# Writing out the engine order ahead of the first block, and loading the first weights deeper

## Chip, cores and metric

One core of one Trainium2 chip. The metric is the device time of one execution in microseconds (us); three runs of the kernel before gave a median of 1016.64 us (1015.66 to 1017.76).

## The reference

Sparse attention over 4 batches and 8 heads of width 64, then two feed-forward networks in a row over 2304 tokens of width 512, all in fp32:

```python
s = scale * q @ k.T          # 512 local tokens: a window of +-32 and 32 global keys
a = exp(s - max(s)); a = a / (sum(a) + 1e-9); x = a @ v
h = x @ w_in;  g = where(h > 0, h, exp(min(h, 0)) - 1);  y = g @ w_out
xn = y / sqrt(mean(y * y) + 1e-6) * rms_g
out = (silu(xn @ w_gate) * (xn @ w_val)) @ w_o2
```

The 32 global tokens of each batch attend to all 544 keys. The weights arrive as 64-bit floats; the kernel gets them as 64-bit integers, turns them into fp32 on the chip, and splits each into a rounded high part and a rest, so that a product is three matmuls.

## The kernel before, in words

**Attention** works on 16 tiles of 128 local tokens, u = 0 to 15. For each, `a_S` (L189) computes scores on TensorE, takes the maxima and scales them on VectorE (L209, L210) and the exponentials on ScalarE (L212). `a_T` (L215) transposes the exponentials on TensorE and copies them on ScalarE (L220). `a_PV` (L223) multiplies with v on TensorE (L235) and divides on VectorE (L239 to L241). `a_X` (L243) transposes the four finished tiles of a block into xT, whose high part ScalarE writes (L250) and whose rest VectorE subtracts (L251).

**Blocks.** `moe_block` (L277) runs the first network over 512 tokens in 16 slots, j = 0 to 15: twelve matmuls for h (`mm1`, L115), the activation (`act1`, L119; in block 0 through `elu_a`, L102), and twelve matmuls into the output sums for the slot before (`mm2`, L129). In blocks 0 to 2 the slots also hold the attention of the four tiles of the next block (`att_slot`, L255), one step each in three slots out of four. Block 3 holds the global tokens. The second network follows.

**Weights.** Sixteen pairs of weight tiles of the first network, in the order of `order1` (L146), are each loaded raw (`dec_load`, L68, 1 MB) and decoded (`decode`, L73): an Abs on ScalarE (L76), four operations on VectorE (L77 to L80), a cast of the high part on ScalarE (L85) and a subtraction on VectorE (L86). The first h needs pairs 0 and 1, the first output sums pair 2; slot 4 needs pairs 4 and 5, slot 8 pairs 8 and 9, slot 12 pairs 12 and 13. Three pairs are decoded ahead of block 0, and one is written into each slot of it after that. The eighteen pairs of the second network (`w2_decode`, L379) are decoded without the split, stored to a DRAM tensor `wT` and read back late in block 3. Both use two buffers for raw tiles (pool `decr`) and two for decoded ones (pool `dec`, tag `dx`). The pool `wpool` has 16 buffers of tag `w`; ahead of block 0 it holds the key/query and value tiles of u = 0 to 3 (`load_kq`, `load_v`, L171 and L180) and later the 16 split weight pairs.

**Order.** TensorE's instructions run in the order in which they are written (L43). The order on VectorE, on ScalarE and of the DMA issues on SP is chosen by a scheduler, which simulates the kernel on a timeline: it gives an engine that it takes to be free the first ready instruction in the order of writing, however far ahead that one was written, if its buffers are free. The order on each engine is fixed once that is done. All loads are issued from SP.

The stretch ahead of block 0 stands at L304 to L370, the slots of block 0 at L388, those of blocks 1 and 2 at L403.

Of the kernel before, what the change touches and what calls it, by code (L numbers as in the profile page):

```python
# [39 lines left out]
def fused_kernel(ctx: ExitStack, tc: tile.TileContext, kq, vl, gkq, gv, w_in, w_out, w_gate, w_val, w_o2, rms_g, consts, out):  # L40
# [27 lines left out]
    def dec_load(pool, src):  # L68
        raw = pool.tile([P, 2, 512], I64, tag="raw", name="raw")
        nc.sync.dma_start(out=raw, in_=src)  # L70
        return raw

    def decode(pool, raw):  # L73
        x = pool.tile([P, 1024], F32, tag="dx", name="dx")
        word = raw.rearrange("p a n -> p (a n)").bitcast(I32).rearrange("p (n w) -> p n w", w=2)
        nc.scalar.activation(x, f(word[:, :, 1]), AF.Abs)  # L76
# [4 lines left out]
        return x  # L81

    def split_w(dst, t):
        t = t.rearrange("p (a n) -> p a n", a=2)
        nc.scalar.copy(dst[:, :, 0, :], t)  # L85
        nc.vector.tensor_tensor(out=dst[:, :, 1, :], in0=t, in1=f(dst[:, :, 0, :]), op=ALU.subtract)  # L86
# [73 lines left out]
    with ExitStack() as ls:  # L160
# [8 lines left out]
        kq_t, v_t, e_t, et_t, x_t = {}, {}, {}, {}, {}  # L169
# [19 lines left out]
        def a_S(u, pools):  # L189
# [12 lines left out]
            for pr in range(4):  # L202
                for par in range(2):
                    r = slice(64 * par, 64 * par + 64)
                    nc.tensor.matmul(ss[par][:, pr, 96:128], t[r, pr, 224:352], t[r, pr, 192:224], start=False, stop=(pr == 3), skip_group_check=True)
            mx = small.tile([P, 2, 4], F32, tag="st", name="mx")
# [16 lines left out]
        def a_PV(u, pools):  # L223
# [3 lines left out]
            if T == 0:  # L227
                x_t[b] = moe.tile([P, 4, 512], F32, tag="x32", name="x")
            x = x_t[b][:, T, :].rearrange("p (a e d) -> p e a d", a=4, e=2)
            os_ = [pools[i][0].tile([P, 4, 65], F32, tag=pools[i][1], name="o") for i in range(2)]  # L230
            st = small.tile([P, 2, 4, 2], F32, tag="st", name="st")
            for par in range(2):
                for pr in range(4):
                    for i in range(4):
                        nc.tensor.matmul(os_[par][32 * i:32 * i + 32, pr, :], ets[par][:, pr * P + 32 * i:pr * P + 32 * i + 32], v[:, i, 2 * pr + par, :],  # L235
                                         start=True, stop=True)
            for par in range(2):
# [17 lines left out]
        def att_slot(b, j, part):  # L255

            u, jj = 4 * (b + 1) + j // 4, j % 4
            if jj == 0 and part == 0:
                a_S(u, ATT2)
                load_kq(u + 1)  # L260
            if jj == 1 and part < 2:
                a_T(u, part, aps, "att")
            if jj == 2 and part == 0:
                a_PV(u, ATT2)
                load_v(u + 1)
# [43 lines left out]
        nc.scalar.copy(identr, ident)  # L309
        nc.scalar.copy(masks, mk)  # L310
        load_v(0)
        load_kq(1)
        nc.vector.memset(eps, 1e-6)

        raws, n_raw, n_dec = [], [0], [0]
# [7 lines left out]
        def w1_decode(n):  # L323
            for _ in range(n):
                i = n_dec[0]
                if i < 16:
                    n_dec[0] += 1
                    t = decode(dec["t"], raws.pop(0))
                    w1_load()
                    kind, a, G = order1[i]  # L330
                    dst = wpool.tile([P, 2, 2, 512], F32R, tag="w", name="wA")
                    for k in range(2):
                        if kind == "1":
                            W1[a + k, G] = dst[:, k]
                        else:
                            W2[a + k] = dst[:, k]
                    split_w(dst, t)
# [12 lines left out]
        load_kq(3)  # L350
        load_v(3)
        a_PV(0, [(yps, "y2"), (yps, "y3")])
        a_S(2, ATT2)
        a_T(1, 0, yps, "y0")
        a_T(1, 1, yps, "y1")
        w1_decode(1)
        nc.sync.dma_start(out=gcol, in_=rms_g.rearrange("(c p) -> p c", p=P))
        a_PV(1, [(yps, "y2"), (yps, "y3")])
        a_S(3, HB)
        a_T(2, 0, yps, "y0")  # L360
        a_T(2, 1, yps, "y1")
        w1_decode(1)
        a_PV(2, [(yps, "y2"), (yps, "y3")])
        a_T(3, 0, yps, "y0")
        a_T(3, 1, yps, "y1")
        a_PV(3, [(yps, "y2"), (yps, "y3")])
        xT_t = {0: new_xT()}
        a_X(0, range(4), xT_t[0], ATT2[:2] + HB)
        load_kq(4)
        load_v(4)  # L370

        raws2, n_raw2, n_dec2 = [], [0], [0]

        def w2_load():
            if n_raw2[0] < 18:
                raws2.append(dec_load(dec["r"], w_src(*order2[n_raw2[0]])))
                n_raw2[0] += 1

        def w2_decode(n):  # L379
            for _ in range(n):  # L380
                i = n_dec2[0]
                if i < 18:
                    n_dec2[0] += 1
                    t = decode(dec["t"], raws2.pop(0))
                    nc.sync.dma_start(out=wT[2 * i:2 * i + 2].rearrange("a p n -> p a n"), in_=t.rearrange("p (a n) -> p a n", a=2))
                    w2_load()

        def slot0(j, part, h):  # L388
            g = act1(h, 512, elu_a) if part == 0 else None
            att_slot(0, j, part)  # L390
            if part == 2:
                w1_decode(1)
# [3 lines left out]
                if j in (13, 15):  # L396
                    w2_decode(1)
# [17 lines left out]
        w2_decode(18)  # L415
# [408 lines left out]
```

## Time and profile before

| | |
|---|---|
| median of 3 runs | 1016.64 us |
| profiled execution | 1016.54 us, span 1014.6 us |
| TensorE matmul busy | 943.7 us, 93% of the span |
| VectorE busy | 457.6 us, 45% |
| ScalarE busy | 348.1 us, 34% |
| mean granted TensorE clock | 0.965 |

Engines are called PE (TensorE matmul), PEld (TensorE weight load), DVE (VectorE), ACT (ScalarE), POOL and SP in the profile; a name with q is the engine's queue. L12 is line 12 of the kernel. All times count from the start of the span. An instruction's row gives its start, its duration, its engine, its line, what it writes and reads, and in brackets how long the engine sat idle before it and who ended that. Clock and DMA share are fractions of the full value.

### The profile page before, as it was taken

The page shows a single profiled execution, that of the slowest core. Times are in us where ns is not written, and L with a number is a line of the kernel's source. Part 1 is how long each engine was busy: PE and PEld are TensorE (multiplying, and loading weights), DVE is VectorE, ACT ScalarE, POOL GpSimd, SP SyncE. Part 2 cuts the span into 40 slices and gives each one's busy share as a digit, 9 for nine tenths or more (in the row PEclk, how much of TensorE's full clock was granted, in tenths as well). Part 3 has the DMA queues.
Part 4 walks back from the last instruction along what each step waited for, and adds up shares of the span by engine and source line. Part 5 has one row for each costly group of instructions (what it writes and reads, how often), then busy time and mean ns, then how long its engine had stood idle before and what let it go on. Part 6 is the DMA issues. An engine that isn't in the chain of part 4 may idle for free.

```text
span 1014.6 us, 15748 instructions
## 1 busy us (share of the span) xinstructions
PE 943.7 (93%) x6738; PEld 781.1 (77%) x6738; DVE 457.6 (45%) x791; ACT 348.1 (34%) x627; POOL 23.7 (2%) x27
## 2 busy tenths in 40 slices
PE   5667898968999999999989999999999999999997
PEld 4545686757887888867777788888888999999996
DVE  3889878877534333443357611412142142142111
ACT  3555645434323232333255522311132142142111
POOL 0000000000000000010010001000100010010000
PEclk9568899989999999999999999999999999999999
DMA  9655687687222212243164400010011001000000
GB/s 354 240 172 209 199 284 276 246 302 272 93 72 69 98 60 72 99 161 125 53 211 135 156 11 1 31 42 1 1 32 42 1 1 63 1 1 32 1 1 32
DMA packets 34446, 107.78 MB, mean 106 GB/s; under 512 B 3016, under 2 KB 5704, under 8 KB 31816
## 3 DMA queue, kind: packets, MB, share of 16 engines
q1 hardware_dynamic: 34376, 106.77, 29.9%
q8 instruction: 53, 0.87, 0.4%
q14 instruction: 17, 0.14, 0.0%
HBM read 88.41 MB, written 18.35 MB: 105 GB/s over the span
## 4 chain that ended last, share of the span: by engine, by line
PE 71%; DMA 11%; DVE 10%; ACT 4%; issue 2%; SPq 1%; ACTq 0%; DVEq 0%
PE pg L561 14%; PE y L567 14%; PE pv L561 14%; PE h L115 11%; PE y L129 11%; DMA raw<-in_moe_w_out 3%; DMA raw<-in_moe_w_in 3%; DMA raw<-in_moe_w_val 3%; DMA raw<-in_moe_w_gate 2%; DVE dx L79 2%; ACT dx L76 2%; DVE dx L80 1%; PE ptp L218 1%; PE o L235 1%; DVE dx L77 1%
## 5 line engine op out<-in xcount | busy, mean ns | idle before, releaser
L129 PE MATMUL y<-g,wA 128*128 128x512 f32 x768 | 205.8, 412 | 6.5 <-ACT g L122 3.3
L115 PE MATMUL h<-xT,wA 128*128 128x512 f32 x768 | 192.6, 400 | 2.8 <-DVE xT L251 2.7
L129 PEld LDWEIGHTS y<-g,wA 128*128 128x128 f32 x768 | 144.1, 195 | 40.8 <-DVE g L123 5.0
L115 PEld LDWEIGHTS h<-xT,wA 128*128 128x128 f32 x768 | 145.9, 192 | 36.6 <-DVE xT L251 3.4
L719 DVE TENSOR_TENSOR silu<-pv,silu 128x384 f32<-128x384 f32 (+1 forms) x60 | 36.7, 611 | 262.2 <-PE pv L561 256.0
L567 PE MATMUL y<-wB,p 128*128 128x512 f32 x612 | 150.7, 393 | 0.0
L567 PEld LDWEIGHTS y<-wB,p 128*128 128x128 f32 x612 | 114.5, 188 | 23.9
L561 PE MATMUL pv<-xT,wB 128*128 128x384 f32 (+1 forms) x432 | 89.0, 354 | 0.0
L718 ACT ACTIVATE silu<-pg 128x384 f32<-128x384 f32 (+1 forms) x60 | 32.1, 534 | 161.3 <-PE pg L561 161.1
L97 DVE TENSOR_SCALAR e<-e 128x512 f32<-128x512 f32 x52 | 22.1, 424 | 134.5 <-ACT e L96 134.5
L561 PEld LDWEIGHTS pv<-xT,wB 128*128 128x128 f32 x432 | 77.7, 188 | 5.9
L721 ACT CAST p<-silu 128x384 fp32r<-128x384 f32 (+1 forms) x60 | 33.4, 557 | 125.7 <-DVE silu L719 125.4
L96 ACT ACTIVATE e<-h 128x512 f32<-128x512 f32 x48 | 28.8, 600 | 118.5 <-PE h L115 109.9
L561 PE MATMUL pv<-xnB,wB 128*128 128x512 f32 (+1 forms) x288 | 61.9, 363 | 0.0
L122 ACT CAST g<-e 128x512 fp32r<-128x512 f32 x64 | 39.7, 620 | 63.2 <-DVE e L98 49.1
L561 PE MATMUL pg<-xT,wB 128*128 128x384 f32 (+1 forms) x288 | 60.4, 358 | 0.0
L76 ACT ACTIVATE dx<-raw 128x1024 f32<-128x1024 f32 x34 | 38.9, 1145 | 61.8 <-DMA raw<-in_moe_w_out 21.4
L561 PEld LDWEIGHTS pv<-xnB,wB 128*128 128x128 f32 x288 | 52.4, 188 | 5.9
L561 PEld LDWEIGHTS pg<-xT,wB 128*128 128x128 f32 x288 | 52.1, 188 | 6.1 <-issue 0.5
L722 DVE TENSOR_TENSOR p<-silu,p 128x384 fp32r<-128x384 f32 (+1 forms) x60 | 37.5, 625 | 35.6 <-ACT p L721 35.6
L123 DVE TENSOR_TENSOR g<-e,g 128x512 fp32r<-128x512 f32 x64 | 44.1, 689 | 19.8 <-ACT g L122 19.1
L218 PE MATMUL ptp<-ident,E 128*128 128x128 f32 x128 | 26.0, 342 | 21.9 <-ACT E L212 21.8
(180 smaller groups left out, 986.5 us busy)
## 6 DMA issues: line engine op xcount, KB each, us to landing
raw<-in_moe_w_out SPq DMA_DIRECT2D x14, 1024.0 KB, 6.1
wT<-dx SPq DMA_DIRECT2D x18, 512.0 KB, 4.2
wraw<-wT SPq DMA_DIRECT2D x18, 512.0 KB, 4.0
raw<-in_moe_w_in SPq DMA_DIRECT2D x8, 1024.0 KB, 6.2
raw<-in_moe_w_gate SPq DMA_DIRECT2D x6, 1024.0 KB, 6.5
raw<-in_moe_w_val SPq DMA_DIRECT2D x6, 1024.0 KB, 8.1
gvr<-in_gv SPq DMA_DIRECT2D x8, 640.0 KB, 5.0
gkq<-in_gkq SPq DMA_DIRECT2D x4, 1152.0 KB, 5.5
```

Source lines behind the costliest of these rows:

```text
L76: nc.scalar.activation(x, f(word[:, :, 1]), AF.Abs)
L115: nc.tensor.matmul(h[:, :n], W1[c, G][:, ws, o:o + P], xT[c][:, xs, :n], start=(k == 0), stop=(k == 11))
L122: nc.scalar.copy(g[:, 0, :n], e[:, :n])
L123: nc.vector.tensor_tensor(out=g[:, 1, :n], in0=e[:, :n], in1=f(g[:, 0, :n]), op=ALU.subtract)
L129: nc.tensor.matmul(ys[dc][:, :n], W2[j][:, ws, dc * P:(dc + 1) * P], g[:, gs, :n], start=(j == 0 and k == 0), stop=(j == 15 and k == 2))
L218: nc.tensor.transpose(pt[:, pr * P:(pr + 1) * P], e_t[u][par][:, pr, :], ident)
L561: nc.tensor.matmul(ps[:, :n], W[c, G3][:, ws, o:o + P], xn[c][:, xs, :n], start=(k == 0), stop=(k == 11))
L567: nc.tensor.matmul(os_[t], p[:, pp, t * P:(t + 1) * P], Wo[j][:, ww, :], start=(j == 0 and k == 0), stop=(j == 11 and k == 2))
L718: nc.scalar.activation(s[:, :n], pg[:, :n], AF.Silu)
L719: nc.vector.tensor_tensor(out=s[:, :n], in0=pv[:, :n], in1=s[:, :n], op=ALU.mult)
L721: nc.scalar.copy(p[:, 0, :n], s[:, :n])
L722: nc.vector.tensor_tensor(out=p[:, 1, :n], in0=s[:, :n], in1=f(p[:, 0, :n]), op=ALU.subtract)
```

## The change

Line numbers after `@@` are of the kernel before.

- `a_S` keeps the scores; the softmax becomes `a_E`. `a_PV` keeps the product; the division becomes `a_N`. `decode` becomes `dec_abs` and `dec_bits`, `split_w` becomes `split_hi` and `split_lo`. What is computed, and how often, stays the same.
- The stretch ahead of block 0 is written out step by step inside a region in which VectorE and ScalarE, too, run in the order of writing. Where instructions that are written outside the region fall among them stays the scheduler's choice, and so does SP's order.
- Raw tiles 1, 3, 5, 7, 9 and 11 go to `wpool` instead of `decr`. Five raw loads are written ahead of the first decode instead of two, two more after the region, and then one after each decode.
- The second weights' decodes are written into the odd slots of blocks 1 and 2 and two more slots of block 2, none in block 0; the first two loads stay in slot 12 of block 0.

```diff
 def w1_load(n=1):
     for _ in range(n):
-        if n_raw[0] < 16:
-            raws.append(dec_load(dec["r"], w_src(*order1[n_raw[0]])))
+        i = n_raw[0]
+        if i < 16:
+            wp = i % 2 == 1 and i < 12
+            raws[i] = dec_load(wpool if wp else dec["r"], "w" if wp else "raw", w_src(*order1[i]))
             n_raw[0] += 1
...
-w1_load(1)
-load_v(1)
-w1_load(1)
-load_kq(2)
-load_v(2)
-a_S(0, ATT2)
-a_S(1, HB)
-a_T(0, 0, yps, "y0")
-a_T(0, 1, yps, "y1")
-w1_decode(1)
-load_kq(3)
-load_v(3)
-a_PV(0, [(yps, "y2"), (yps, "y3")])
...
+with tc.manual_schedule(engines={mybir.EngineType.DVE, mybir.EngineType.Activation}):
+    nc.scalar.copy(identr, ident)
+    nc.scalar.copy(masks, mk)
+    load_kq(1)
+    w1_load()
+    load_v(1)
+    w1_load()
+    load_kq(2)
+    load_v(2)
+    load_kq(3)
+    load_v(3)
+    w1_load(3)
+    a_S(0, ATT2)
+    a_E(0)
+    a_S(1, HB)
+    w1_abs(0)
+    a_T(0, 0, yps, "y0")
+    a_T(0, 1, yps, "y1")
+    w1_bits(0)
+    a_E(1)
+    a_PV(0, Y2)
+    w1_hi(0)
+    a_N(0)
+    w1_lo(0)
+    a_S(2, ATT2)
+    w1_abs(1)
+    a_T(1, 0, yps, "y0")
+    a_T(1, 1, yps, "y1")
+    a_E(2)
+    w1_bits(1)
+    a_PV(1, Y2)
+    w1_hi(1)
+    a_N(1)
+    a_S(3, HB)
+    a_T(2, 0, yps, "y0")
+    a_T(2, 1, yps, "y1")
+    a_E(3)
+    w1_lo(1)
+    a_PV(2, Y2)
+    a_N(2)
+    w1_abs(2)
+    a_T(3, 0, yps, "y0")
+    a_T(3, 1, yps, "y1")
+    w1_bits(2)
+    a_PV(3, Y2)
+    a_N(3)
+    w1_hi(2)
+    xT_t = {0: new_xT()}
+    a_X(0, (0, 1), xT_t[0], ATT2[:2] + HB)
+    w1_lo(2)
+    a_X(0, (2, 3), xT_t[0], ATT2[:2] + HB)
+w1_load(2)
 load_kq(4)
 load_v(4)
+nc.sync.dma_start(out=gcol, in_=rms_g.rearrange("(c p) -> p c", p=P))
...
 if part == 2:
-    w1_decode(1)
+    w1_decode()
     if j == 12:
         w2_load()
         w2_load()
-    if j in (13, 15):
-        w2_decode(1)
...
 if part == 2:
-    w2_decode(1 if j % 2 else 0)
+    if j % 2 or (b == 2 and j in (4, 10)):
+        w2_decode()
...
-w2_decode(18)
+assert n_dec2[0] == 18
```

## Rows read from the trace of the kernel before

**Rows 1.** Chain of waits that ended last, shares of the span by engine.

```profile
PE 71%; DMA 11%; DVE 10%; ACT 4%; issue 2%; SPq 1%; ACTq 0%; DVEq 0%
```

**Rows 2.** Busy time by stage: PE, PEld, DVE, ACT, POOL, clock, DMA share, GB/s.

```profile
12.30:65.90 53.60, 32.81 (x551) 25.00 (x550) 43.06 (x77) 29.37 (x58) 0.00 (x0) 0.65 0.69 261
65.90:121.50 55.60, 44.88 (x377) 35.80 (x378) 49.93 (x67) 31.68 (x54) 0.00 (x0) 0.84 0.58 198
121.50:194.00 72.50, 69.06 (x630) 54.83 (x628) 59.12 (x92) 38.62 (x66) 0.00 (x0) 1.00 0.79 274
194.00:262.00 68.00, 56.71 (x490) 44.39 (x489) 50.71 (x80) 25.85 (x46) 0.00 (x0) 0.92 0.73 259
...
321.00:430.90 109.90, 109.46 (x1018) 88.68 (x1017) 42.36 (x96) 35.16 (x78) 0.00 (x0) 1.00 0.23 82
```

**Rows 3.** Timeline of TensorE, first matmuls of blocks 0, 1, 2: start, us.

```profile
65.91 4.72 PE L115 MATMUL h<-xT,wA 128*128 128x512 f32 x12 [2.35 <-DVE xT L251]
...
194.00 2.81 PE L115 MATMUL h<-xT,wA 128*128 128x512 f32 x10
...
321.00 2.88 PE L115 MATMUL h<-xT,wA 128*128 128x512 f32 x12
```

**Rows 4.** Groups by line up to 66 us: busy, mean ns | idle before.

```profile
L79 DVE SCALAR_TENSOR_TENSOR dx<-raw,dx 128x1024 int32<-128x1024 int32 x7 | 8.5, 1216 | 0.0
...
L86 DVE TENSOR_TENSOR wA<-dx,wA 128x1024 fp32r<-128x1024 f32 x6 | 7.3, 1220 | 0.8 <-ACT wA L85 0.8
...
L209 DVE TENSOR_REDUCE mx<-s 128x4 f32<-128x512 f32 x8 | 5.3, 684 | 11.5 <-PE s L205 11.5
...
L77 DVE TENSOR_SCALAR dx<-dx 128x1024 f32<-128x1024 f32 x7 | 4.8, 691 | 9.2 <-ACT dx L76 9.2
...
L241 DVE TENSOR_TENSOR x<-o,st 128x256 f32<-128x256 f32 x8 | 3.3, 418 | 0.1
...
L251 DVE TENSOR_TENSOR xT<-xtp,xT 128x512 fp32r<-128x512 f32 x4 | 2.6, 682 | 0.0
...
L210 DVE TENSOR_SCALAR mx<-mx 128x4 f32<-128x4 f32 x8 | 1.1, 162 | 0.0
```

**Rows 5.** Timeline of all engines ahead of block 0.

```profile
12.23 1.22 PE L195 MATMUL s<-masks,identr 128*128 128x512 f32 x2
...
14.65 1.12 ACT L76 ACTIVATE dx<-raw 128x1024 f32<-128x1024 f32 x1 [6.93 <-DMA raw<-in_moe_w_in]
...
14.85 1.92 PE L205 MATMUL s<-kq 64*128 64x32 f32 x16
...
17.28 2.17 ACT L212 ACTIVATE E<-s,mx 128x128 f32<-128x128 f32 x8 [1.50 <-DVE mx L210]
...
22.33 1.96 PE L235 MATMUL o<-v,ET 128*32 128x65 f32 x64 [2.35 <-ACT ET L220]
...
31.51 1.12 ACT L76 ACTIVATE dx<-raw 128x1024 f32<-128x1024 f32 x1 [1.45 <-DMA raw<-in_moe_w_out]
...
60.52 3.04 PE L249 MATMUL xtp<-ident,x 128*128 128x128 f32 x13 [6.01 <-DVE x L241]
```

**Rows 6.** Who waited for whom in block 0: us, times, longest.

```profile
PE ptp L218 <- ACT E L212: 11.9, 3, 7.5
```

**Rows 7.** Timeline of ScalarE in block 0, an Abs and the exponentials.

```profile
112.99 1.14 ACT L76 ACTIVATE dx<-raw 128x1024 f32<-128x1024 f32 x1 [3.36 <-DMA raw<-in_moe_w_out]
114.03 2.14 ACT L212 ACTIVATE E<-s,mx 128x128 f32<-128x128 f32 x8
```

**Rows 8.** Timeline of ScalarE: sixteenth Abs, first and last of 18 second ones.

```profile
121.30 1.12 ACT L76 ACTIVATE dx<-raw 128x1024 f32<-128x1024 f32 x1 [0.94 <-DMA raw<-in_moe_w_out]
...
125.64 1.14 ACT L76 ACTIVATE dx<-raw 128x1024 f32<-128x1024 f32 x1
...
253.10 1.14 ACT L76 ACTIVATE dx<-raw 128x1024 f32<-128x1024 f32 x1 [0.77 <-DMA raw<-in_moe_w_out]
```

**Rows 9.** Busy time by stage, columns as in rows 2, 10 to 20 us.

```profile
10.00:20.00 10.00, 9.04 (x130) 6.81 (x116) 4.85 (x8) 3.57 (x10) 0.00 (x0) 1.00 1.02 422
```

More of the change, by code (lines that the diff above doesn't have):

```diff
@@ L59, in fused_kernel, with dec_load, words, dec_abs @@
     wT = dram.tile([36, P, 512], F32, name="wT")
[L68 to L69 removed]
+    def dec_load(pool, tag, src):
+        raw = pool.tile([P, 2, 512], I64, tag=tag, name="raw")
         nc.sync.dma_start(out=raw, in_=src)
         return raw
[L73 removed]
+    def words(raw):
+        return raw.rearrange("p a n -> p (a n)").bitcast(I32).rearrange("p (n w) -> p n w", w=2)
+    def dec_abs(pool, raw):
         x = pool.tile([P, 1024], F32, tag="dx", name="dx")
[L75 to L76 removed]
+        nc.scalar.activation(x, f(words(raw)[:, :, 1]), AF.Abs)
+        return x
+    def dec_bits(x, raw):
+        word = words(raw)
         nc.vector.tensor_scalar(out=x, in0=x, scalar1=HI_MIN, scalar2=HI_MAX, op0=ALU.max, op1=ALU.min)
@@ L236, in a_PV, with a_N @@
                                          start=True, stop=True)
+            o_t[u] = os_
+        def a_N(u):
+            b, T = u // 4, u % 4
+            if T == 0:
+                x_t[b] = moe.tile([P, 4, 512], F32, tag="x32", name="x")
+            x = x_t[b][:, T, :].rearrange("p (a e d) -> p e a d", a=4, e=2)
+            os_ = o_t.pop(u)
+            st = small.tile([P, 2, 4, 2], F32, tag="st", name="st")
             for par in range(2):
@@ L259, in att_slot @@
                 a_S(u, ATT2)
+                a_E(u)
                 load_kq(u + 1)
@@ L321, in w1_load @@
                     n_raw[0] += 1
[L323 to L337, printed above, removed]
@@ new lines, in w1_hi, with w1_lo, w1_decode @@
+        def w1_hi(i):
+            kind, a, G = order1[i]
+            dst = wpool.tile([P, 2, 2, 512], F32R, tag="w", name="wA")
+            for k in range(2):
+                if kind == "1":
+                    W1[a + k, G] = dst[:, k]
+                else:
+                    W2[a + k] = dst[:, k]
+            split_hi(dst, dxs[i])
+            dsts[i] = dst
+        def w1_lo(i):
+            split_lo(dsts.pop(i), dxs.pop(i))
+            n_dec[0] = i + 1
+        def w1_decode():
+            i = n_dec[0]
+            if i < 16:
+                w1_abs(i)
+                w1_bits(i)
+                w1_hi(i)
+                w1_lo(i)
+                w1_load()
@@ L375, in w2_load, with w2_decode @@
             if n_raw2[0] < 18:
-                raws2.append(dec_load(dec["r"], w_src(*order2[n_raw2[0]])))
+                raws2.append(dec_load(dec["r"], "raw", w_src(*order2[n_raw2[0]])))
                 n_raw2[0] += 1
[L379 to L386, printed above, removed]
+        def w2_decode():
+            i = n_dec2[0]
+            if i < 18:
+                n_dec2[0] += 1
+                raw = raws2.pop(0)
+                t = dec_abs(dec["t"], raw)
+                dec_bits(t, raw)
+                nc.sync.dma_start(out=wT[2 * i:2 * i + 2].rearrange("a p n -> p a n"), in_=t.rearrange("p (a n) -> p a n", a=2))
+                w2_load()
         def slot0(j, part, h):
```

48 lines of the change are left out of this document (19 added, 29 removed).

## The prediction

> **What bounds the kernel now.** I read the chain of waits first. It lies on TensorE for 71% of the span, but DMA has 11% and VectorE 10% [rows 1], so somewhere the kernel waits for weights to arrive and be decoded. The table by stage shows where [rows 2]. Its pieces are the stretch ahead of block 0, block 0 in two parts, the first part of block 1, and block 2. Block 2, 109.9 us, has TensorE busy for 109.46 and is what a block costs when nothing else is in its way. The stretch ahead of block 0 has TensorE busy for 32.81 of 53.6 us at a mean granted clock of 0.65. Block 0 starts at 65.91 us, block 1 at 194.00 and block 2 at 321.00 [rows 3], so block 0 takes 128.1 and block 1 127.0 us. Block 0 has one group of twelve output matmuls fewer than block 2 (twelve matmuls of this size: 2.88 us, rows 3), so its floor is 107.0. The losses against the floors are 21.1 us in block 0 and 17.1 us in block 1; after 321 us there is nothing for this change to win.
>
> Why the early stretch is long stands in the groups by line up to 66 us [rows 4]: seven decodes have reached L79's step there and six their last one, L86, though only three are written ahead of block 0. The scheduler fills VectorE with decodes as soon as it thinks that it is free, and the attention steps queue behind them. The timeline shows one such step [rows 5]: TensorE is done with the scores of tile 0 and goes on to tile 1 at 12.23 us, but ScalarE does the decode's Abs first, at 14.65, after waiting 6.93 us for its DMA, and the exponentials start at 17.28 only. The last transposes wait 6.01 us for VectorE's x.
>
> **Part 1, the written order.** I follow the new order through the engines, with the durations of this trace. One decode is 0.69 + 0.69 + 1.22 + 1.22 + 1.22 = 5.04 us of VectorE (two of the L77 kind, two of the L79 kind, one L86) and one Abs of 1.12 on ScalarE [rows 4, 5]. A tile's softmax (two maxima of 0.68 and two scalings of 0.16) is 1.7 us of VectorE; the division (two products of 0.42 and four small operations, which I put at the 0.16 of L210) is 1.5. On TensorE a tile's scores take 4.55 us (12.23 to 16.77), P times V 1.96, the eight exponentials on ScalarE 2.17 [rows 5]; the eight transposes and their second copy I put at 2.8 together. This comes out, in us from the start:
> - tile 0: exponentials 13.2 to 15.5; Abs 0 from 15.5 (its data is there at 14.65); decode 0 on VectorE 16.6 to 20.4; P times V 19.6 to 21.6; end of decode 0 at 25.7.
> - tile 1: softmax on VectorE 20.4 to 22.1, behind decode 0; exponentials until 23.5; scores of tile 2 on TensorE 21.6 to 26.1; P times V of tile 1 28.9 to 30.9; decode 1 on VectorE 27.8 to 31.6.
> - tile 2: scores of tile 3 30.9 to 35.4; transposes and copies to 38.1; exponentials of tile 3 38.1 to 40.3; P times V 38.1 to 40.1; Abs 2 at 40.3; decode 2 on VectorE 41.6 to 45.4, behind the division of tile 2.
> - tile 3: P times V 43.1 to 45.1; division to 46.9; four times four transposes, the last decode step (1.2), and three of the four 0.68 us subtractions of L251 until the score buffer that the first matmul of block 0 reuses is free: 51.8 us.
>
> Against 65.91 that is 14.1 us earlier. The written order fixes only what is written inside it: decode 3, written in block 0, can still be put between its instructions, because its load no longer waits for a buffer. That costs from 0 up to the 5.0 us of one whole decode, as the two decode buffers hold no more; I take 1.6, since VectorE has gaps of about 2 us ahead of the third tile's division and of the transposes. **Term 1: 12.5 us gained, ends 9 and 14.**
>
> **Part 2, five loads.** The raw tiles 1 and 3 go into weight buffers that are empty then, so they wait for no decode. The new order sends two key/query and value tiles (kq and v of tile 3) ahead of raw 2, and raw 2 ahead of kq and v of tile 4. Raw 2 came at 31.51 before [rows 5], behind about the same bytes, and is wanted at 40.3: no wait, worth nothing here by itself. On SP nothing is queued behind a wait but raw 4, which waits for decode 0 at 20.4, and it is wanted in block 0. In block 0 the depth counts. TensorE lost 11.9 us there in three waits for the exponentials, 7.5 the longest [rows 6]. One of them is plain to see: Abs waits 3.36 us for its load, and the exponentials stand right behind it on ScalarE [rows 7]. With four raw tiles ahead this cause goes; the other one, maxima queued behind decode steps on VectorE, stays. Of the 21.1 us of loss the first six slots have 55.6 - (6 x 6.87 - 2.9) = 17.3, and the rest 3.8 [rows 2]. The cold start of the first matmuls stays (4.72 against 2.88, rows 3); with half of the 11.9, 6, and 4 of smaller waits, 12 of the 21.1 stay. **Term 2: 9 us gained, ends 17 and a loss of 10** (the loss is the give-back below).
>
> Is block 0 fed in time when it starts with 3 decoded tiles instead of 6? The sixteen Abs of the first weights lie between 14.65 and 121.30 [rows 5, 8], a pace of 7.1 us. Slot 4 needs two more tiles after 3, so six in all, slot 8 ten, slot 12 fourteen. At that pace from 51.8 they are there at 73, 101 and 130 us; at 6.87 us a slot, TensorE wants them at 76, 104 and 131. So it holds even at the old pace, by 1 to 3 us. VectorE's work in block 0 doesn't grow: 13 x 5.04 = 66 us against some 9 x 5.04 + 9 x 3.82 = 80.
>
> **Part 3, the second weights.** Eighteen decodes of four VectorE steps (3.82 us) stay; before, they ran from 125.64 to 253.10, nine in block 0 and nine in block 1 [rows 8], though eight are written in block 2. They ran far ahead of where they were written, and I see no reason why this should stop: the scheduler still fills free time. The nine in block 0 cost 3.8 us of TensorE, 0.4 each; the nine in block 1 17.1, 1.9 each. The raw tiles of these stay two deep, and each load is written on SP behind a store that waits for the decode before it. Since the first weights now take more of block 0, I expect about three there and fifteen after. At 0.4 each, 18 cost 8; at 1.9 each, 34; they cost 21 now. **Term 3: nothing, ends 13 gained and 13 lost.** What is late next in block 1 is the exponentials again, behind an Abs that waits.
>
> **The sum.** The profiled execution took 1016.54 us for a span of 1014.6, so 1.9 lie around it, and the median of the runs is 1016.64, the same within 0.1. 1016.5 - 12.5 - 9 - 0 = 995.
>
> **The rivals.**
> - *The second weights spread out.* If they do land as written, eight in block 1 and ten in block 2, block 1 loses little: 995 - 13 = 982. For it: VectorE has less free time in block 0. Against it: before, the first ran at 125.64, in slot 6, though it is written in slot 13 [rows 8].
> - *The gain is given back.* Block 0 starts earlier with fewer weights and waits for decodes. The margin is 1 to 3 us at a pace of 7.1; at 8 us a decode, the fourteenth is there at 140 instead of 131, and block 0 loses 10 against term 2: 1005.
> - *Slower: the head of ScalarE's line.* An Abs of a tile outside the written order is placed ahead of the exponentials of tile 1 (due at 21.3 us), while raw 4 can't be issued before decode 0 is through at 20.4. By the tiles' shapes kq is 0.72 MB, v 1.06, raw 1.05. Raw 2 was the last of 10.5 MB of loads and came at 31.51 [rows 5]; in the new order it ends the same bytes, with raw 3 behind it, then raw 4, or kq and v of tile 4 and raw 5 (2.8 MB) and then raw 4. At 422 GB/s [rows 9], 2.5 us for a raw tile, it lands at 36.5 to 43. The whole written order then waits 15 to 22 us; with 18.5, the middle, block 0 starts at 71.9, 6 later than now, and with no more tiles decoded it gains nothing: 1022. It decides from a wait of 14 us on. Against it: the wait at 14.65, 6.93 us, was mostly spent before anything else was ready. How such a wait is passed on is seen in block 0, where the Abs at 112.99 holds the exponentials to 114.03 [rows 7]. [...]
> - *No change.* The scheduler fills the new order with as many decodes as the old: 1016.
>
> **How the numbers follow.** Forecast 0.5, spread out 0.2, given back 0.18, slower 0.07, no change 0.05. Range: the three faster cases with their bounds, 978 to 1008. A measurement of this kernel tells about 0.2% (2 us) from no change. Faster 0.88, same 0.04, slower 0.08.
>
> **What would show it.** Right: in the timeline the first exponentials start near 13 us and the first h matmul near 53; at most four tiles have reached L86's operation by then; TensorE's waits for exponentials in block 0 fall from 11.9 us to about 6; block 0 is near 119 and block 1 near 127; block 2 stays at 110. Wrong: an h matmul waiting for wA (given back), an Abs of the fourth or fifth raw tile ahead of tile 1's exponentials (slower), w_gate loads only after the start of block 1 (spread out).

## The result, and the profile after

The median went from 1017.19 us (4 runs, 1015.66 to 1017.76) to 993.77 us (4 runs, 992.05 to 994.95): a ratio of 0.9771, 95% interval 0.9751 to 0.979. The profiled execution took 994.44 us for a span of 992.4. The forecast was 995. The total was right; where the time came from was right only ahead of block 0, and the total agrees in part by luck: block 0 gave nothing where 9 us were forecast, and block 1 gave 8.4 where nothing was.

Line numbers are each kernel's own. In the kernel after, L78 is the Abs, L86 the fourth decode step, L92 the split's subtraction, L223 and L224 the maxima and their scaling, L226 the exponentials, L232 the transposes of the softmax, L260 the division, L270 the last subtraction ahead of a block.

The page of the kernel after, its span and the shares of the chain of waits:

```profile
span 992.4 us, 15749 instructions
...
PE 72%; DVE 13%; DMA 7%; ACT 5%; issue 2%; SPq 0%; ACTq 0%; DVEq 0%
```

DMA has gone from 11% to 7% of the chain, VectorE from 10% to 13% [rows 1]: fewer steps end by waiting for a raw tile, more by waiting for VectorE. The same table by stage as [rows 2], of the kernel after (PE, PEld, DVE, ACT and POOL busy, clock, DMA share, GB/s):

```profile
12.30:51.00 38.70, 26.43 (x549) 21.69 (x548) 33.05 (x64) 25.29 (x54) 0.00 (x0) 0.78 0.91 357
51.00:97.80 46.80, 42.42 (x377) 33.56 (x378) 46.60 (x65) 31.12 (x51) 0.00 (x0) 0.93 0.53 189
97.80:180.40 82.60, 72.73 (x630) 57.03 (x629) 69.46 (x104) 44.41 (x73) 0.00 (x0) 0.96 0.69 244
180.40:299.00 118.60, 112.23 (x1018) 89.65 (x1017) 77.05 (x134) 44.84 (x87) 0.00 (x0) 0.98 0.57 197
299.00:408.80 109.80, 109.36 (x1017) 88.61 (x1016) 42.28 (x96) 35.10 (x78) 0.00 (x0) 1.00 0.23 82
```

Block 0 starts at 51.0 instead of 65.9. Its first six slots take 46.8 instead of 55.6, but its last ten 82.6 instead of 72.5, and there TensorE is idle for 9.9 us where it was idle for 3.4; the rest of these 10.1 us is the same work at a lower clock (busy for 72.73 us at a granted clock of 0.96, where it was 69.06 at 1.00). Block 1 takes 118.6 instead of 127.0; block 2 is unchanged. By the floors of the prediction (107.0 and 109.9) block 0 loses 22.4 and block 1 8.7, where it was 21.1 and 17.1.

The timeline of TensorE of the kernel after, the first matmuls of blocks 0 and 1, as in [rows 3], and ahead of them the transposes that wait for the division:

```profile
44.89 3.04 PE L268 MATMUL xtp<-ident,x 128*128 128x128 f32 x13 [4.17 <-DVE x L260]
...
51.01 4.61 PE L125 MATMUL h<-xT,wA 128*128 128x512 f32 x12 [3.09 <-DVE xT L270]
...
180.37 3.22 PE L125 MATMUL h<-xT,wA 128*128 128x512 f32 x12
```

The 4.17 us wait is for VectorE, and the timeline of VectorE shows what it did meanwhile: the two costliest steps of a decode that is written outside the region, and the division of the last tile behind them.

```profile
41.28 1.22 DVE L85 SCALAR_TENSOR_TENSOR dx<-raw,dx 128x1024 int32<-128x1024 int32 x1
42.53 1.23 DVE L86 SCALAR_TENSOR_TENSOR dx<-raw,dx 128x1024 int32<-128x1024 int32 x1
43.67 0.42 DVE L260 TENSOR_TENSOR x<-o,st 128x256 f32<-128x256 f32 x1
```

The groups by line up to 51 us of the kernel after, which answer to [rows 4]: four decodes have reached their last step (L92, which was L86 before), where six had.

```profile
L92 DVE TENSOR_TENSOR wA<-dx,wA 128x1024 fp32r<-128x1024 f32 x4 | 4.9, 1222 | 1.0 <-ACT wA L89 1.0
```

The timeline of ScalarE of the kernel after, which answers to [rows 5, 8]: the first exponentials, the first Abs, the sixteenth, the first of the eighteen of the second weights, one in block 0's last slot, and the last.

```profile
12.29 2.18 ACT L226 ACTIVATE E<-s,mx 128x128 f32<-128x128 f32 x8 [5.61 <-DVE mx L224]
14.30 1.18 ACT L78 ACTIVATE dx<-raw 128x1024 f32<-128x1024 f32 x1
...
113.53 1.19 ACT L78 ACTIVATE dx<-raw 128x1024 f32<-128x1024 f32 x1 [3.32 <-DMA raw<-in_moe_w_out]
119.47 1.14 ACT L78 ACTIVATE dx<-raw 128x1024 f32<-128x1024 f32 x1 [2.29 <-DMA raw<-in_moe_w_gate]
...
171.62 1.12 ACT L78 ACTIVATE dx<-raw 128x1024 f32<-128x1024 f32 x1 [4.27 <-DMA raw<-in_moe_w_gate]
...
243.88 1.13 ACT L78 ACTIVATE dx<-raw 128x1024 f32<-128x1024 f32 x1
```

The second weights run from 119.47 to 243.88, nine in block 0 and nine in block 1. They are written from block 1 on and still start in block 0.

Who waited for whom in block 0 of the kernel after (us in total, times, longest), which answers to [rows 6]:

```profile
ACT dx L78 <- DMA raw<-in_moe_w_out: 9.8, 4, 3.8
PE ptp L232 <- ACT E L226: 8.7, 4, 3.8
ACT dx L78 <- DMA raw<-in_moe_w_gate: 7.3, 4, 4.3
ACT dx L78 <- DMA raw<-in_moe_w_val: 4.4, 2, 2.7
```

TensorE's waits for exponentials are at 8.7 us in place of 11.9, and ScalarE still waits for raw tiles, 21.5 us in all, where it was 25.5 before. Of the 8.7 us, 3.85 fall into slot 1. In slot 15, 14.1 us long, the Abs at 171.62 stands for 4.27 us, the casts of xT stand behind it, and TensorE waits for xT twice, 2.28 and 1.68 us.

### The profile page after: what moved, and what is told of

The parts are those of the page before. It is cut to its first block, busy times and chain, and to the rows that moved or that the text cites. A ratio compares the mean times of both kernels' runs of the same rounds, so it can differ in the third digit from the quotient of the medians.

```text
span 992.4 us, 15749 instructions
## 1 busy us (share of the span) xinstructions
PE 936.4 (94%) x6738; PEld 776.4 (78%) x6738; DVE 458.5 (46%) x791; ACT 348.9 (35%) x627; POOL 23.8 (2%) x27
## 4 chain that ended last, share of the span: by engine, by line
PE 72%; DVE 13%; DMA 7%; ACT 5%; issue 2%; SPq 0%; ACTq 0%; DVEq 0%
PE pv L623 14%; PE pg L623 14%; PE y L629 14%; PE h L125 11%; PE y L139 11%; DMA raw<-in_moe_w_val 2%; DMA raw<-in_moe_w_out 2%; DVE dx L86 2%; DVE dx L85 2%; ACT dx L78 1%; DVE dx L83 1%; DVE wA L92 1%; ACT E L226 1%; DVE wB L92 1%; DVE g L133 1%
## 5 line engine op out<-in xcount | busy, mean ns | idle before, releaser
L78 ACT ACTIVATE dx<-raw 128x1024 f32<-128x1024 f32 x34 | 39.4, 1162 | 42.8 <-DMA raw<-in_moe_w_out 14.9
L226 ACT ACTIVATE E<-s,mx 128x128 f32<-128x128 f32 x128 | 34.9, 383 | 24.2 <-DVE mx L224 24.0
```

Source lines behind the costliest of these rows:

```text
L78: nc.scalar.activation(x, f(words(raw)[:, :, 1]), AF.Abs)
L226: nc.scalar.activation(e[par][:, pr, :], ss[par][:, pr, :], AF.Exp, bias=mx[:, par, pr:pr + 1], scale=SCALE)
```

## The experiments

The question was what each of the three parts had given, and what keeps blocks 0 and 1 above their floors. All stages are read from the profiled executions, from the first h matmul of a block to the next one's, and medians and ratios from the timed runs; a profiled execution can lie some 2 us off its median (e10: 1003.65 and 1001.43). Two theories of the remaining loss stood against each other after the first four runs: that the decodes cost by VectorE's time, wherever they are put, or that they cost where an Abs waits at the head of ScalarE's line for a load.

| kernel | block 0 starts | block 0 (first 6 + last 10 slots) | block 1 | block 2 | from block 3 | median | ratio (95%) |
|---|---|---|---|---|---|---|---|
| before | 65.9 | 128.1 (55.6 + 72.5) | 127.0 | 109.9 | 583.7 | 1017.19 | |
| after | 51.0 | 129.4 (46.8 + 82.6) | 118.6 | 109.9 | 583.6 | 993.77 | 0.9771 (0.9751 to 0.979) |
| e1 | 52.7 | 130.6 (46.7 + 83.9) | 125.1 | 109.9 | 584.6 | 1004.47 | 0.988 (0.9861 to 0.99) |
| e2 | 62.4 | 126.9 (49.5 + 77.4) | 125.8 | 109.7 | 585.1 | 1013.23 | 0.9972 (0.9951 to 0.9994) |
| e3 | 51.1 | 131.2 (46.8 + 84.4) | 119.4 | 109.9 | 583.5 | 995.1 | 0.9786 (0.976 to 0.9812) |
| e4 | 51.3 | 118.7 (46.8 + 71.9) | 125.3 | 121.7 | 583.6 | 1002.57 | 0.9863 (0.9844 to 0.9883) |
| e5 | 50.7 | 120.7 (46.8 + 73.9) | 110.5 | 110.5 | 594.5 | 989.57 | 0.9729 (0.9709 to 0.9748) |
| e6 | 45.7 | 125.5 (50.4 + 75.1) | 127.5 | 109.9 | 583.8 | 994.58 | 0.9777 (0.9759 to 0.9795) |
| e7 | 45.4 | 121.4 (50.5 + 70.9) | 111.5 | 111.9 | 595.1 | 986.95 | 0.9702 (0.9681 to 0.9723) |
| e8 | 50.9 | 119.6 (46.8 + 72.8) | 116.2 | 109.9 | 583.6 | 983.07 | 0.9658 (0.9633 to 0.9684) |
| e9 | 45.8 | 121.4 (50.4 + 71.0) | 116.1 | 110.3 | 584.6 | 981.19 | 0.9642 (0.9617 to 0.9667) |
| e10 | 51.3 | 132.4 (54.4 + 78.0) | 124.5 | 110.0 | 583.1 | 1001.43 | 0.9842 (0.9815 to 0.987) |

**e1: the written order alone.** From the kernel after: all raw tiles in `decr`, two ahead, and the second weights written as before.

```diff
-            wp = i % 2 == 1 and i < 12
+            wp = False
...
-    w1_load(3)
...
     w1_bits(0)
+    w1_load()
...
     w1_bits(1)
+    w1_load()
...
     w1_bits(2)
+    w1_load()
...
-w1_load(2)
...
+    if j in (13, 15):
+        w2_decode()
...
-    if j % 2 or (b == 2 and j in (4, 10)):
+    if j % 2:
         w2_decode()
```

> The written order ahead of block 0 alone: raw tiles in two buffers as before, each load written after a decode, second weights written as before. Theory A (the order gives the 14.9 us ahead of block 0, the depth of the loads the 8.8 us in its first six slots, the place in which the second weights are written nothing): block 0 starts at 50 to 53 us, its first six slots take 52 to 57 us instead of 46.8, and the total is near 1002. Theory B (the order gives both, the depth is worth nothing): total 992 to 995, first six slots near 47 us. Theory C (the order is worth little without the deeper loads, because its decodes wait for raw tiles): block 0 starts after 60 us, total above 1007.

1004.47 us. By its ratio the order alone gains 1.2%, 12 us (10 to 14). It gives 13.2 of the 14.9 us ahead of block 0, as theory A had it, and all of the gain in the first six slots (46.7), as theory B had it. What five loads add to it, 1004.47 - 993.77 = 10.7 us (9.4 against e3, in which the second weights are written as in e1), lies for 6.5 in block 1 and for 1.2 in block 0.

The reason is in the waits of e1 from 52.8 to 308 us, its blocks 0 and 1 (us in total, times, longest):

```profile
ACT dx L78 <- DMA raw<-in_moe_w_out: 21.4, 9, 4.3
...
ACT dx L78 <- DMA raw<-in_moe_w_val: 13.2, 4, 4.2
ACT dx L78 <- DMA raw<-in_moe_w_gate: 7.9, 6, 2.8
...
ACT dx L78 <- DMA raw<-in_moe_w_in: 6.2, 4, 2.3
```

and in those of the kernel after from 51 to 299 us, blocks 0 and 1 again:

```profile
ACT dx L78 <- DMA raw<-in_moe_w_out: 14.9, 6, 4.1
...
ACT dx L78 <- DMA raw<-in_moe_w_gate: 12.1, 6, 4.3
ACT dx L78 <- DMA raw<-in_moe_w_val: 10.0, 5, 4.3
```

Abs waits for loads for 48.7 us in e1 and for 37.0 after, and the waits on `w_in` are gone. All thirty-four decodes stand in one stream; with the deeper queue the last Abs comes at 243.88 instead of 254.6, and so much less of the stream lies in block 1.

**e2: five loads alone.** From the kernel before: odd raw tiles below 12 in `wpool`, kq and v of tile 3 and three loads written behind `load_v(2)`.

```diff
-            raws.append(dec_load(dec["r"], w_src(*order1[n_raw[0]])))
+            wp = n_raw[0] % 2 == 1 and n_raw[0] < 12
+            raws.append(dec_load(wpool if wp else dec["r"], w_src(*order1[n_raw[0]]), "w" if wp else "raw"))
...
 load_v(2)
+load_kq(3)
+load_v(3)
+w1_load(3)
...
-load_kq(3)
-load_v(3)
```

> The kernel before with only the deeper loads: raw tiles 1, 3, 5, 7, 9, 11 in weight buffers, five loads written ahead of the first decode; order left to the scheduler, second weights as before. Theory A: block 0 starts near 66 us, its first six slots take 45 to 49 us instead of 55.6, total near 1008. Theory B: block 0 starts near 66, first six slots 55, total near 1016. Theory C: part of the gain ahead of block 0 appears too, start below 60 us, total near 1000.

1013.23 us, a gain of 0.28%, 3 us (0.6 to 5). Alone the depth gives 3, on top of the order 10.7; the parts are worth 12 and 3 singly and 23 together. None of the three theories fits: block 0 starts at 62.4 and its first six slots take 49.5, so depth alone gives 3.5 us ahead of block 0 and 6.1 in those slots too, but the last ten lose 4.9. Why order and depth help each other by 8 us is not taken apart further.

**e3: the second weights written where they were before.** From the kernel after.

```diff
+    if j in (13, 15):
+        w2_decode()
...
-    if j % 2 or (b == 2 and j in (4, 10)):
+    if j % 2:
         w2_decode()
```

> The changed kernel with the second weights written where they were before (slots 13 and 15 of block 0, odd slots of blocks 1 and 2). Theory A: the scheduler places them by free time and not by where they are written, so the total stays at 994 within 1 us, with nine of the eighteen Abs in block 0 as now. Rival (the writing does move them or their cost): 996 to 1004, with the loss in block 1 back at 17 us.

995.1 us against 993.77, with intervals that overlap for the most part, and the stages agree within 1.8 us; nine second decodes fall into block 0, as theory A said. Where the second weights are written is worth nothing that can be measured, because they run ahead of either place.

**e4: the second weights' loads held back.** Each load waits for the `g` of the slot in which it is written, by a one-element write of GpSimd into the raw tile, so the decodes land in blocks 1 and 2 (Abs from 168 to 393 us: one in the last slot of block 0, eight in block 1, nine in block 2).

```diff
-        raws2.append(dec_load(dec["r"], "raw", w_src(*order2[n_raw2[0]])))
+        raw = dec["r"].tile([P, 2, 512], I64, tag="raw", name="raw")
+        nc.gpsimd.tensor_copy(raw.rearrange("p a n -> p (a n)").bitcast(I32)[0:1, 0:1], i32(held[0][0:1, 0, 0:1]))
+        nc.sync.dma_start(out=raw, in_=w_src(*order2[n_raw2[0]]))
...
-    if j == 12:
-        w2_load()
+    if j >= 14:
         w2_load()
```

> The changed kernel with the loads of the second weights held back for real: a one-element copy on GpSimd from the activation of the slot into the raw tile goes ahead of each load, so loads start in slots 14 and 15 of block 0 and then one in each slot with a decode; eight decodes fall into block 1 and ten into block 2. Theory D (the second weights cost TensorE most where they compete with the first ones on VectorE and where two are squeezed into little time): the last ten slots of block 0 lose 2 to 6 us instead of 13.9, block 1 and block 2 lose under 5 each, total 978 to 985. Rival E (a second-weight decode costs about 1.2 us wherever it stands): block 0 gains 10, blocks 1 and 2 lose as much again, total 991 to 996. Rival F (holding them starves something late, or delays the read-back in block 3): above 996.

1002.57 us: slower than the kernel after by 8.8, in the range of rival F but not by its delay in block 3, since the stretch from block 3 on is unchanged. Block 0 falls to 118.7, since it is rid of all but one of the second weights, but block 1 rises to 125.3 and block 2 to 121.7, 15.4 and 11.8 over the floor, though neither holds more than nine of them. Most of the loss stands in slots 1, 5, 9 and 13, in which transposes wait for exponentials: 8.6, 12.8, 8.3 and 9.4 us in block 1, 10.1, 10.3, 8.4 and 8.6 in block 2, against 6.4 or 6.5 undisturbed. Slots 6, 8 and 10, in which Abs stand too, take 6.8, 8.1 and 6.8, as they do without. The timeline of all engines of e4 around one such slot:

```profile
203.18 0.38 SPq L442 DMA_DIRECT2D raw<-in_moe_w_val  x1
...
204.09 1.08 PE L215 MATMUL s<-kq__1891 64*128 64x32 f32 x16
...
208.12 1.13 ACT L78 ACTIVATE dx<-raw 128x1024 f32<-128x1024 f32 x1 [4.65 <-DMA raw<-in_moe_w_val]
209.14 0.62 ACT L132 CAST g<-e 128x512 fp32r<-128x512 f32 x1
209.28 0.69 DVE L83 TENSOR_SCALAR dx<-dx 128x1024 f32<-128x1024 f32 x1 [4.62 <-ACT dx L78]
...
211.09 1.28 DVE L223 TENSOR_REDUCE mx<-s 128x4 f32<-128x512 f32 x2
...
213.68 2.17 ACT L226 ACTIVATE E<-s,mx 128x128 f32<-128x128 f32 x8 [3.92 <-DVE mx L224]
...
214.88 1.11 PE L232 MATMUL ptp<-ident,E 128*128 128x128 f32 x4 [4.06 <-DVE dx L86]
```

The load is issued at 203.18 and the Abs stands at the head of ScalarE's line for 4.65 us until its data is there at 208.12. VectorE stands for the same time at L83, which needs that Abs. The scores are done at 205.17, but the maxima stand behind L83 on VectorE and start at 211.09, and the activation's cast stands behind the Abs. A decode step of 1.21 us (L85) comes between the maxima and their scaling as well. The exponentials start at 213.68, and TensorE waits 4.06 us. (The profile puts this wait down to the decode step that ended beside them, L86; the transposes read the exponentials.) The wait costs more than itself, as the stage of this slot shows:

```profile
207.90:220.70 12.80, 8.74 (x33) 6.94 (x33) 7.36 (x12) 5.98 (x14) 0.70 (x1) 0.73 0.25 88
```

The granted clock is 0.73 in the mean, and TensorE is busy for 8.74 us in a slot that takes 6.4 in all where nothing waits. In blocks 1 and 2 together its waits at these transposes are 18.2 us and its busy time is 7.7 us above twice that of block 2 in [rows 2], of the 27.2 us lost. So one late load held two engines at once, ScalarE for 4.65 us and VectorE for 4.62, and what was queued behind waited on both: the cast, whose input was there at 204.66, starts at 209.14, when the Abs is through, and the maxima, whose scores were done at 205.17, at 211.09, behind L83. In slot 1 of block 1, where the Abs waits 1.55 us only, decode steps ahead of the maxima, and between them and the scaling, still come with a wait of 2.01 on TensorE.

**e5: the Abs held back, the loads free.** From the kernel after: each second Abs waits for the `g` of its slot, and the decodes are written into slots without exponentials. The load then has a slot's time or more to arrive.

```diff
-def dec_abs(pool, raw):
+def dec_abs(pool, raw, hold=None):
     x = pool.tile([P, 1024], F32, tag="dx", name="dx")
+    if hold is not None:
+        nc.gpsimd.tensor_copy(i32(x[0:1, 0:1]), i32(hold))
...
-    t = dec_abs(dec["t"], raw)
+    t = dec_abs(dec["t"], raw, held[0][0:1, 0, 0:1])
...
+    if j >= 14:
+        w2_decode()
...
-    if j % 2 or (b == 2 and j in (4, 10)):
+    if j % 4 >= 2:
         w2_decode()
```

> The changed kernel with the Abs of each second-weight decode held back instead of its load: a one-element copy on GpSimd from the activation of the slot into the decoded tile goes ahead of the Abs. Two decodes fall into slots 14 and 15 of block 0, eight into block 1 and eight into block 2, all in the two slots of four in which no exponentials are due; a raw tile then has two to four slots to land. Theory G (a second-weight decode costs TensorE time only where its Abs waits for its load, or stands, ahead of the exponentials in ScalarE's order): the last ten slots of block 0 take 70 to 74 us instead of 82.6, block 1 110 to 113, block 2 110 to 112, ScalarE's waits for gate, value and output loads fall below 3 us, total 975 to 981. Rival E (a decode costs TensorE about 1.2 us wherever it stands, by VectorE's time): total 990 to 1000. Rival H (the cost is VectorE's alone, but only next to the division in slot 2 of four): 982 to 989.

989.57 us. Blocks 0 to 2 come out as theory G said, the total does not. Its stages for blocks 1 and 2:

```profile
171.40:281.90 110.50, 109.63 (x1017) 88.55 (x1016) 70.90 (x126) 43.54 (x87) 5.17 (x8) 1.00 0.55 190
281.90:392.50 110.60, 109.73 (x1018) 88.58 (x1018) 70.90 (x126) 43.69 (x88) 5.17 (x8) 1.00 0.48 169
```

Eight decodes in a block now cost 0.6 us, with VectorE as busy as in block 1 of the kernel after within 10% (70.90 and 77.05). TensorE waits for no exponentials at all in these two blocks, where it waited 18.2 us in blocks 1 and 2 of e4 (eight waits), and ScalarE waits for no load there. So VectorE's time as such is not the price. Nor is it every decode that meets a softmax in its queues. The timeline of all engines of e5 around the end of slot 4 of block 1 (slot 5 starts at 206.24):

```profile
204.50 1.22 DVE L88 SCALAR_TENSOR_TENSOR dx<-raw,dx 128x1024 int32<-128x1024 int32 x1
...
206.23 1.28 DVE L225 TENSOR_REDUCE mx<-s 128x4 f32<-128x512 f32 x2
...
207.69 2.18 ACT L228 ACTIVATE E<-s,mx 128x128 f32<-128x128 f32 x8 [2.45 <-DVE mx L226]
...
209.00 0.60 PE L234 MATMUL ptp<-ident,E 128*128 128x128 f32 x4
```

The scores are done at 203.50, and the last decode step stands ahead of the maxima. The exponentials start 1.45 us into slot 5, some 1.9 us later than in block 2 of the kernel after, where no decode is about and they start 7.5 us into slot 4, of 8.0. Yet the transposes, due 2.8 us into slot 5, don't wait. In slot 5 of e4 the exponentials start 5.74 us into the slot, and TensorE waits 4.06. So a decode cost here what it made a softmax late beyond the 2 us or so that the softmax could spare; the 2 us are an estimate from these rows. e5 takes away both the wait for the load and the decode steps among the softmax's own, and how much is due to each isn't separated. But the stretch from block 3 on takes 10.9 us more. Its timeline of TensorE and of the DMA issues on SP names the reason:

```profile
400.10 0.34 SPq L677 DMA_DIRECT2D gkq<-in_gkq  x1
...
405.35 1.16 PE L696 MATMUL gs<-gkq 64*32 64x272 f32 x16 [9.97 <-DMA gkq<-in_gkq]
```

The global tokens' keys are issued at 400.10, 7.6 us after block 3 began at 392.46, and TensorE waits 9.97 us for them. In the kernel after they are issued at 398.12, 10.7 us ahead of block 3. Who waited for whom on SP from 370 to 410 us of e5:

```profile
SPq L677 <- DMA wT<-dx: 2.4, 1, 2.4
```

The issue of the keys waits for the landing of the last decode's store, which itself was issued only at 397.04, when the last decode was done.

**e6: no fill.** From the kernel after: the Abs of decodes 3 and 4 wait for the last copy ahead of block 0.

```diff
-            dxs[i] = dec_abs(dec["t"], raws[i])
+            dxs[i] = dec_abs(dec["t"], raws[i], xlast[0:1, 1, 0:1] if i in (3, 4) else None)
```

> The changed kernel with the Abs of first-weight decodes 3 and 4 held until the last part of xT is written, so that nothing from outside the written order falls among its instructions. Theory I (the filled-in decodes cost the stretch ahead of block 0 nearly their whole VectorE time, and block 0 gets it back only in part): block 0 starts at 45 to 48 us instead of 51.0, block 0 takes 1 to 4 us longer, total 989 to 993. Rival J (the time is conserved: what the stretch gains, block 0 loses waiting for decodes): start 45 to 48, block 0 4 to 7 us longer, total 993 to 996. Rival K (the fill lies in gaps and costs nothing): start 50 to 51, total 994 or above.

The timeline of TensorE of e6, the first h matmuls:

```profile
45.71 2.50 PE L127 MATMUL h<-xT,wA 128*128 128x512 f32 x5 [1.43 <-DVE xT L272]
```

Block 0 starts 5.3 us earlier than in the kernel after, yet the median is 994.58, the same, above theory I's range. Block 0 takes 3.9 less too, and block 1 takes 8.9 more (127.5): the last Abs is still at 246 us. The stream of decodes doesn't end sooner because block 0 begins sooner, so more of it falls into block 1: eleven second decodes instead of nine. The time is given back, as in rival J, but in block 1 and not in block 0.

**e7: e5 and e6 together.**

> The edits of the two runs above together. If they act on different stretches, the gains add up: by theories G and I 970 to 979; by G and J 975 to 983; by E and J 990 or above.

986.95 us. With the Abs held, 2.6 us of the 5.3 are kept. The stretch from block 3 on is as long as in e5 (595.1), which no sum had allowed for, and the total lies above 983.

**e8: e5 with the decodes done early.** From e5: one more second decode in block 0, eleven in block 1, four in block 2, the last in slot 7.

```diff
-    if j >= 14:
+    if j >= 13:
         w2_decode()
...
-    if j % 4 >= 2:
+    if (j % 4 >= 2 or j in (1, 5, 9)) if b == 1 else j in (2, 3, 6, 7):
         w2_decode()
```

> The kernel with the held Abs, its second weights done earlier: three decodes in block 0 (slots 13 to 15), eleven in block 1, four in block 2 up to slot 7 instead of eight up to slot 15. Theory L (the 10.9 us that the run before lost after block 2 come from the first load of the global tokens' keys, whose buffers are those of the decodes, so that it can start only when the last decode is stored): the stretch from block 3 on takes 583 to 585 us instead of 594.5, blocks 1 and 2 110 to 113, total 977 to 982. Rival (the loss has another cause, such as the order on SP or the copies on GpSimd): the stretch stays at 592 to 596, total 988 to 992.

983.07 us, and 583.6 from block 3 on, as in the kernel after. The timeline of SP of e8:

```profile
385.75 0.33 SPq L677 DMA_DIRECT2D gkq<-in_gkq  x1
```

So the late end of the decodes made e5's 10.9 us, as theory L said; the total is 1 us above its range, by block 1. With the wait of SP in e5 it speaks for the buffers: there the issue of the keys waited 2.4 us for the last store to land. Block 1 pays 6 us for eleven decodes where eight cost 0.6; its slots 2, 3 and 13 are the long ones (7.2, 9.2, 7.5). Slots 1, 5 and 9 hold exponentials and now decodes too, and take 6.4, 6.4 and 6.8: an Abs held to the `g` of its slot comes behind that slot's exponentials (in e9, whose block 1 is written the same way, the exponentials in slots 1, 5 and 9 start at 175.47, 207.12 and 235.00 us, the Abs at 186.44, 212.43 and 240.31).

**e9: e8 and e6 together.**

> The same with the Abs of first-weight decodes 3 and 4 held as well until xT is written. By the runs so far the earlier start (45.4) costs block 0 little (121.4 against 120.7): total 2 to 6 us under the run beside it, 972 to 978. Rival: the time is conserved, the same total within 1 us.

981.19 us, the fastest of all: 12.6 us under the kernel after, and 1.9 under e8, just less than the 2 to 6 expected. In its chain of waits DMA is down to 2%. What is left over the floors is 14.4 us in block 0 and 6.2 in block 1.

**e10: the kernel before without fill.** From the kernel before, no order written, two loads: the Abs of decodes 3 and 4 wait for the last copy ahead of block 0.

```diff
-                    t = decode(dec["t"], raws.pop(0))
+                    t = decode(dec["t"], raws.pop(0), xlast[0][0:1, 1, 0:1] if i in (3, 4) else None)
```

> The kernel before with one edit: the Abs of first-weight decodes 3 and 4 held until xT is written, so that the scheduler can't fill decodes of block 0 into the stretch ahead of it; the order of the rest stays the scheduler's. Theory M (what the written order gains ahead of block 0 is mostly that fewer decodes fall into the stretch): block 0 starts at 48 to 54 us instead of 65.9, total 1003 to 1010. Rival N (it is the order of the attention steps among the decodes that counts, fill or not): block 0 starts at 58 to 66, total 1010 to 1020.

The first h matmul of e10 in the timeline of TensorE:

```profile
51.33 3.02 PE L117 MATMUL h<-xT,wA 128*128 128x512 f32 x12 [1.29 <-DVE xT L253]
```

and the fourth decode step in its groups by line up to there, three of them where six had run before:

```profile
L82 DVE SCALAR_TENSOR_TENSOR dx<-raw,dx 128x1024 int32<-128x1024 int32 x3 | 3.7, 1220 | 0.0
```

Block 0 starts at 51.3, as with the whole written order, and the median is 1001.43, 16.7 us under the 1018.1 of the kernel before that ran beside it. Two held instructions, with no other edit, give 14.6 us ahead of block 0, and block 0 gives back 4.3 of them. The start is as theory M said, the total a little better. With no fill the written order and the deeper queue together bring block 0 another 5.6 forward (45.7, e6).

## Why the prediction was right, and where it was wrong

**What bounds the kernel** was read rightly: fill decodes queued ahead of attention steps make the stretch ahead of block 0 long. e10 shows it alone, without any of the change: 16.7 us, where the whole change gave 23.4. Of the signs named, those ahead of block 0 came out (first exponentials at 12.29, first h matmul at 51.01, four decodes through); the others did not: TensorE's waits for exponentials in block 0 are 8.7 us and not about 6, block 0 takes 129.4 and not 119, block 1 118.6 and not 127.

**Term 1 (12.5 forecast, 14.9 measured) was near by two errors that cancel.** The worked-out chain without fill ended at 51.8; e6, which has no fill, starts at 45.7. The fill was put at 1.6, with an end at 5.0; it takes 51.0 - 45.7 = 5.3, past that end: besides decode 3, two steps of decode 4 have run by then. The first error is in the durations: the prediction gave each tile's scores the 4.55 us that tile 1 took before. In the kernel after those of tile 2 take 3.5 and those of tile 3 2.7; the last section has more on it. P times V of tile 0 comes 2 us earlier than worked out as well (17.55 against 19.6). The exponentials of tile 3, put at 38.1, start at 33.16. The second is in the place of the fill: it was put into VectorE's gaps, but it came ahead of the last division, where no gap was (the 4.17 us wait at 44.89).

**Term 2 (9 forecast in block 0) has its size by luck and not its place.** Five loads are worth about 10 us on top of the order, but block 0 as a whole lost 1.3. "12 of the 21.1 stay" would have made block 0 119; it took 129.4. The first six slots did gain 8.8, but the order alone gives that too (e1: 46.7), and the depth alone 6.1 of it (e2). "With four raw tiles ahead this cause goes" did not hold: ScalarE's waits for raw tiles fell from 25.5 to 21.5 us only. The last ten lost 10.1. The step that failed is "I expect about three there and fifteen after": the first weights' Abs came at 6.6 us each instead of 7.1 and ended at 113.53, ahead of the 121.30 of before, so nine second decodes fell into block 0 again. VectorE's work in block 0, which "doesn't grow" by the forecast, grew from 109.1 to 116.1 us. With all but one of them held out of it (e4) block 0 takes 118.7, the 119 of the forecast.

**Term 3 (nothing) held as a sum and not in its prices.** The nine in block 0 were put at 0.4 us each. They cost 82.6 - 71.9 = 10.7, 1.2 each, by the comparison with e4, and the nine in block 1 8.7, 1.0 each and not 1.9. The late part of block 0 and block 1 together lost 20.9 before and 22.6 after. e3 shows the edit itself to be worth nothing. Seventeen of the same eighteen cost 27.2 in blocks 1 and 2 of e4, and sixteen of them 1.2 in e5, so a price per decode was the wrong thing to take from the trace: the price depended on how late a decode made a softmax (in slot 5 of block 1 the exponentials start 5.74 us into the slot in e4, with a wait of 4.06 on TensorE, and 1.45 in e5, with none).

**Block 0 is fed in time**, as worked out: among TensorE's waits in block 0 none is for wA.

**The rivals.** *Spread out* (982) did not happen, and e4 shows that it would not have given 982: forced into blocks 1 and 2, with Abs that wait for their loads, the decodes make 1002.57. e8 comes to 983.07 with spreading, but only as the Abs don't wait. *Given back* (1005) did not happen by its mechanism; something else gave back 10.1 us late in block 0, the second weights. *Slower* (1022): the Abs of the fourth raw tile stands behind the exponentials of tile 3, at 36.20, and no wait came ahead of tile 1's. Its mechanism is real, though: e4 shows it in blocks 1 and 2, where an Abs stood for 4.65 us and TensorE then waited 4.06 for the exponentials. In the case that the prediction gave for it, the Abs of [rows 7] held the exponentials for about 0.3 us only, since the scaling ahead of them ended at 113.71. That a written order passes on 15 to 22 us of such a wait whole was the author's estimate; no run shows it. *No change* (1016) is excluded by the interval.

**What stays open.** Slot 1 of block 0 takes 12.2 us in the kernel after (9.4 in e3, whose edit doesn't touch it) and 6.4 in block 1, and no run touched it alone. That order and depth help each other is measured, not explained, and so is that nine second decodes in block 0 went with a loss of 3.8 us in its last ten slots before and of 13.9 after.

## What to carry to other kernels

A scheduler that fills free time with later work can put that work into a latency chain: look at how many steps of later work have been done when the chain ends, and hold those few back, before an order is written out by hand. An instruction that needs a load should be placed where the load has already landed; in e4 a late one kept ScalarE standing for 4.65 us, with the cast that was queued behind the Abs, and VectorE, which takes the output of that Abs, for 4.62. What that cost here was what went beyond the time that the work behind could spare, some 2 us by the estimate from e4 and e5. When the start of a stage is brought forward, ask whether the stream that feeds the next one ends any sooner, since otherwise the gain is paid back there.

## What the runs showed of the hardware that was not expected

Scores of one tile took 4.55 us in the kernel before (tile 1, which the prediction went by) and 2.7 in the kernel after (tile 3). The timeline of TensorE of the kernel after, the first and last groups of tile 3's scores:

```profile
26.13 0.72 PE L205 MATMUL s<-masks,identr 128*128 128x512 f32 x2
...
27.71 1.08 PE L215 MATMUL s<-kq 64*128 64x32 f32 x16
```

For tile 1 before, the two groups took 1.22 and 1.92 [rows 5]. But the trace of before has both durations itself. Its timeline of TensorE, the last groups of tiles 2 and 3:

```profile
26.26 1.08 PE L205 MATMUL s<-kq 64*128 64x32 f32 x16
...
37.66 1.92 PE L205 MATMUL s<-kq 64*128 64x32 f32 x16
```

The granted clock is 1.00 from 25.3 to 28.6 us of that trace, and 0.50 from 35 to 40. The table by stage of the kernel after shows a like change, in the column after the busy times:

```profile
20.00:30.00 10.00, 8.02 (x240) 6.07 (x238) 8.65 (x19) 7.31 (x20) 0.00 (x0) 1.00 1.01 407
30.00:51.00 21.00, 10.71 (x156) 8.86 (x156) 19.37 (x40) 13.64 (x23) 0.00 (x0) 0.59 0.82 310
```

From 20 to 30 us the clock is at 1.00, and TensorE is busy for 8.02 of 10 us; from 30 to 51, where it is busy for 10.71 of 21, it is at 0.59 in the mean. For tile 1 before, the column says 1.00 as well [rows 9], against the long durations. There is no record behind it: the records of the granted clock begin at 25.2 us in the trace of before and at 20.5 in that of after, and ahead of them the column shows 1.00. That tile 1 ran at 0.50 is argued from its durations, which are those of tile 3 at 0.50, and is not shown. So a chain worked out with one duration for each kind of step, read at one place of the trace, did not hold in a stretch in which the granted clock is 1.00 in one part and 0.50 in another.
